# Layer 2 of an attention + two-layer MLP kernel: plain block products against one-level Strassen on 768-token groups

## The chip, the cores and the metric

The kernel runs on one core of a Trainium2 chip. The metric is the device time of one execution in microseconds (us).

## What is computed

Attention with a causal mask and a cumulative bias over 4 batches, 8 heads, 576 positions and head size 64, then two MLP layers on the 2304 tokens (d_model 512, d_ff 2048):

```python
x = attn_out.transpose(0, 2, 1, 3).reshape(2304, 512)
h = x @ w_in;    x = (h * clip(h + 3, 0, 6) / 6) @ w_out      # layer 1
h = x @ w2_in;   y = (h * tanh(log1p(exp(h)))) @ w2_out       # layer 2
```

All inputs are float32. The kernel keeps the precision with pairs of float32r tiles: each operand is split into a high part (a rounding cast) and a low part (the difference), and a product is three matmuls, high x high, high x low and low x high (`TERMS`). The weights arrive as 64-bit words and are rebuilt to float32 on the chip.

## The kernel before, in words

Tokens are processed in five blocks, `BLOCKS` (line 24), of 512 or 384 columns. A step is one block with one of the 16 slices `f` of d_ff. In `moe_step` (line 726) a step of layer 2 does G1, line 735: 4 chunks of d_model x 3 terms = 12 matmuls of N columns into one PSUM bank; then Mish on ScalarE (line 753), the high cast (line 755, made by `copy`, line 303 or 307) and the low difference on VectorE (line 756); then G2, line 773: N/128 x 3 matmuls of 512 columns that accumulate over the 16 slices in PSUM. Layer 1 has the same form with lines 735 and 768; its G2 has 4 x 3 matmuls of N columns. G1 of a later step stands between the groups of G2 of an earlier one, three matmuls by three.

`load_split` (line 341) brings a slice of weights (512 KB of words, `wraw`), rebuilds it in four VectorE or ScalarE operations (`wtmp`, lines 352 to 368) and splits it (lines 377 and 378). Layer 1's `w_out` slices are written to DRAM (`wos`, line 403) and read again per step into three `wo` buffers (line 406). Layer 2's slices all stay on the chip.

The order of each engine's work is made ahead of time by a planner (`Plan`, line 67) from costs, priorities and due times (table `T`, line 34). Attention (`unit` and `small`) runs beside layer 1: its operations on VectorE, ScalarE and GpSimd stand between the MLP's. During the first part of the program the planner fills idle time of TensorE with dummy matmuls (`warm`, line 293).

## Time and profile before

| what | us |
|---|---|
| median of 3 runs | 1002.57 (1002.32 to 1002.92) |
| profiled execution, first to last instruction (span) | 999.2 |
| TensorE busy in it | 987.7 |
| VectorE busy | 462.9 |
| ScalarE busy | 475.6 |
| GpSimd busy | 44.4 |

For the profiled execution the profile gives the span and no other time; the 3.4 us between it and the median of the runs is what lies around the span. A busy time counts an engine while any of its instructions is open. A matmul's own duration is longer than the distance from its start to the next one's start, because matmuls overlap in the engine; the pace is read from starts. VectorE operations overlap by their ends in the same way.

### The profile page before, as it was taken

The page shows a single profiled execution, that of the slowest core. Times are in us where ns is not written, and L with a number is a line of the kernel's source. Part 1 is how long each engine was busy: PE and PEld are TensorE (multiplying, and loading weights), DVE is VectorE, ACT ScalarE, POOL GpSimd, SP SyncE. Part 2 cuts the span into 40 slices and gives each one's busy share as a digit, 9 for nine tenths or more (in the row PEclk, how much of TensorE's full clock was granted, in tenths as well). Part 3 has the DMA queues.
Part 4 walks back from the last instruction along what each step waited for, and adds up shares of the span by engine and source line. Part 5 has one row for each costly group of instructions (what it writes and reads, how often), then busy time and mean ns, then how long its engine had stood idle before and what let it go on. Part 6 is the DMA issues. An engine that isn't in the chain of part 4 may idle for free.

```text
span 999.2 us, 14034 instructions
## 1 busy us (share of the span) xinstructions
PE 987.7 (99%) x5142; PEld 810.7 (81%) x5142; DVE 462.9 (46%) x1067; ACT 475.6 (48%) x1008; POOL 44.4 (4%) x102
## 2 busy tenths in 40 slices
PE   8899999999999999999999999999999999999998
PEld 6567777777777898888889998888888888888996
DVE  7898888754544455435228789612112112111111
ACT  5887777766655565544226556313223223222222
POOL 2111110101011001000000000000000000000000
PEclk9999999999999999999999999999999999999999
DMA  8786876887566766466237775202001102000101
GB/s 276 221 251 223 277 242 229 262 262 223 170 202 201 236 211 207 146 230 221 90 121 258 258 269 177 81 1 74 1 1 43 43 1 63 1 1 1 43 1 32
DMA packets 60356, 146.06 MB, mean 146 GB/s; under 512 B 8352, under 2 KB 22720, under 8 KB 60288
## 3 DMA queue, kind: packets, MB, share of 16 engines
q1 hardware_dynamic: 60288, 145.17, 44.8%
q8 instruction: 41, 0.67, 0.3%
q14 instruction: 27, 0.22, 0.1%
HBM read 121.84 MB, written 23.31 MB: 145 GB/s over the span
## 4 chain that ended last, share of the span: by engine, by line
PE 97%; DVE 2%; ACT 1%; issue 0%; POOL 0%; POOLq 0%; DVEq 0%; ACTq 0%
PE b L735 40%; PE b L768 21%; PE b L773 20%; PE b L499 4%; PE b L568 4%; PE b L545 3%; PE b L623 2%; PE b L293 1%; PE b L677 1%; PE b L668 1%; DVE g L635 0%; ACT cb L642 0%; DVE wtmp L362 0%; DVE cb L635 0%; DVE win L378 0%
## 5 line engine op out<-in xcount | busy, mean ns | idle before, releaser
L735 PE MATMUL b<-blk,win 128*128 128x512 f32 (+1 forms) x1920 | 505.3, 373 | 0.0
L735 PEld LDWEIGHTS b<-blk,win 128*128 128x128 f32 x1920 | 347.1, 188 | 58.0 <-issue 6.9
L768 PE MATMUL b<-g,wo 128*128 128x512 f32 (+1 forms) x960 | 258.6, 377 | 0.0
L768 PEld LDWEIGHTS b<-g,wo 128*128 128x128 f32 x960 | 170.3, 188 | 28.4 <-issue 8.2
L756 DVE TENSOR_TENSOR g<-e,g 128x512 fp32r<-128x512 f32 (+1 forms) x120 | 77.0, 642 | 215.4 <-ACT g L303 214.4
L753 ACT ACTIVATE e<-b 128x512 f32<-128x512 f32 (+1 forms) x80 | 44.4, 555 | 249.2 <-PE b L735 249.0
L773 PE MATMUL b<-wo,wo 128*128 128x512 f32 x432 | 122.0, 391 | 0.0
L773 PE MATMUL b<-wo,g 128*128 128x512 f32 x432 | 122.0, 391 | 0.0
L303 ACT ACTIVATE g<-e 128x512 fp32r<-128x512 f32 (+1 forms) x105 | 62.2, 593 | 78.4 <-PE b L768 76.8
L773 PEld LDWEIGHTS b<-wo,g 128*128 128x128 f32 x432 | 80.5, 188 | 13.3 <-DVE g L756 0.3
L773 PEld LDWEIGHTS b<-wo,wo 128*128 128x128 f32 x432 | 80.6, 188 | 12.9
L756 DVE TENSOR_TENSOR wo<-e,wo 128x512 fp32r<-128x512 f32 (+1 forms) x40 | 25.5, 638 | 131.6 <-ACT wo L303 131.4
L748 DVE SCALAR_TENSOR_TENSOR e<-e,b 128x512 f32<-128x512 f32 (+1 forms) x80 | 50.4, 629 | 59.4 <-ACT e L746 58.5
L514 ACT ACTIVATE cb<-cb,nm 128x384 f32<-128x384 f32 (+2 forms) x80 | 54.4, 682 | 29.7 <-DVE nm L506 29.0
L746 ACT ACTIVATE e<-b,three 128x512 f32<-128x512 f32 (+1 forms) x80 | 51.4, 642 | 32.3 <-DVE g L756 16.2
L506 DVE CUSTOM_DVE_ANT_0 cb<-b,cb 128x384 f32<-128x384 f32 (+2 forms) x80 | 44.7, 588 | 29.6 <-PE b L499 25.6
L303 ACT ACTIVATE pt<-b 128x384 f32<-128x384 f32 (+2 forms) x95 | 47.8, 504 | 19.5 <-PE b L545 18.5
L545 PE MATMUL b<-ident,cb 128*128 128x128 f32 x304 | 48.8, 272 | 0.0
L545 PEld LDWEIGHTS b<-ident,cb 128*128 128x128 f32 x304 | 39.0, 140 | 9.2
L499 PE MATMUL b<-qk 64*128 64x384 f32 (+2 forms) x288 | 46.2, 364 | 0.0
L362 DVE SCALAR_TENSOR_TENSOR wtmp<-wraw,wtmp 128x512 uint32<-128x512 uint32 x64 | 44.2, 691 | 1.2
L368 DVE SCALAR_TENSOR_TENSOR wtmp<-wraw,wtmp 128x512 uint32<-128x512 uint32 x64 | 44.0, 687 | 1.0
(79 smaller groups left out, 744.0 us busy)
## 6 DMA issues: line engine op xcount, KB each, us to landing
wo<-wos SPq DMA_DIRECT2D x64, 512.0 KB, 3.7
wraw<-in_w_in_dram SPq DMA_DIRECT2D x32, 512.0 KB, 4.9
wraw<-in_w_out_dram SPq DMA_DIRECT2D x32, 512.0 KB, 4.4
cb<-cuml SPq DMA_DIRECT2D x16, 896.0 KB, 7.6
wos<-wo SPq DMA_DIRECT2D x16, 512.0 KB, 4.9
qkr<-in_qk_dram SPq DMA_DIRECT2D x16, 480.0 KB, 3.6
v<-in_v_dram SPq DMA_DIRECT2D x16, 320.0 KB, 6.4
cb<-cums SPq DMA_DIRECT2D x12, 384.0 KB, 4.5
```

The costliest lines, as they stand in the source:

```text
L303: nc.scalar.activation(out=out_, in_=in_, func=AF.Copy)
L499: nc.tensor.matmul(out=ps[g].t[:, 0:w], lhsT=t.t[s_, ka, qo:qo + P], rhs=t.t[s_, kb, nk0 + a:nk0 + e], start=k == 0, stop=k == 2)
L506: nc.vector.tensor_tensor_reduce(out=p.t[:, o:o + w], in0=pb.t[:, 0:w], in1=cb.t[:, o:o + w], scale=-0.125, scalar=(3.0e38 if a == 0 else ...
L514: nc.scalar.activation(out=p.t[:, o:o + w], in_=p.t[:, o:o + w], func=AF.Exp, scale=-1.0, bias=nm.t[:, k:k + 1], accum_out=l.t[:, k:k + 1],)
L545: nc.tensor.transpose(out=ps.t[:, P * z:P * (z + 1)], in_=p.t[:, o:o + P], identity=ident)
L735: nc.tensor.matmul(out=hps.t[:, 0:N], lhsT=w.t[:, a, P * c:P * (c + 1)], rhs=x.t[:, c, b, :], start=(c == 0 and k == 0), stop=(c == NCC - ...
L746: a = add("ACT", actp(N, 1), lambda: nc.scalar.activation(out=e0.t[:, 0:N], in_=hps.t[:, 0:N], func=AF.Relu, bias=three, scale=1.0), [prev ...
L748: a = add("DVE", v1x(N), lambda: nc.vector.scalar_tensor_tensor(out=e0.t[:, 0:N], in0=e0.t[:, 0:N], scalar=6.0, in1=hps.t[:, 0:N], op0=ALU ...
L753: a = add("ACT", actp(N) + 0.15, lambda: nc.scalar.activation(out=e0.t[:, 0:N], in_=hps.t[:, 0:N], func=AF.Mish), [prev], t, [e0], [hps])
L756: gl = add("DVE", v1x(N), lambda: nc.vector.tensor_tensor(out=g.t[:, 1, 0:N], in0=src.t[:, 0:N], in1=r(g.t[:, 0, 0:N]), op=ALU.subtract), ...
L768: nc.tensor.matmul(out=y[j].t[:, 0:N], lhsT=wt.t[:, a, P * j:P * (j + 1)], rhs=g.t[:, b, 0:N], start=(f == 0 and k == 0), stop=(f == NF - ...
L773: nc.tensor.matmul(out=y[j].t, lhsT=g.t[:, a, P * j:P * (j + 1)], rhs=wt.t[:, b, :], start=(f == 0 and k == 0), stop=(f == NF - 1 and k == 2),
```

## The change

Layer 2 is computed on three groups of 768 tokens (`SUPER`), each group in a G1 part and then a G2 part. In both parts the matrices are cut into 2 x 2 blocks: d_model into halves, d_ff into halves (slice `f` with slice `f + 8`), tokens into halves of 384 (`NS`). Seven block products with sums of blocks take the place of eight (the Winograd form). In G1 a product is 6 matmuls of 384 columns for one of 8 slice pairs; in G2 it is 8 x 6 matmuls over the slice pairs, into two banks. One chain (`last_pe`) sets the order of the products on TensorE.

- **Weights.** `combine_in` (for `w2_in`) and `combine` (for `w2_out`) rebuild two slices, form the block sums with four VectorE operations of 256 columns, and write seven blocks to DRAM (`wss`): `w2_in` as float32 (three writes, 896 KB for a slice pair), `w2_out` split already (one write of 1792 KB). The first runs beside attention, the second late in layer 1. `granule` reads one block per product: 128 KB in G1, split on the chip, 256 KB in G2.
- **Tokens.** `operands` reads layer 1's output of the group, forms four sums and splits seven operands of 768 columns. In G2 `op` forms sums of the Mish outputs for four of the seven products and splits each operand of 384 columns.
- **Partial results.** A bank is read (`snap`, a copy, or `psum_add`) in the middle of its accumulation, and later products go on accumulating in it.
- **Layer 1 and attention** keep their work. The planner's table `T` has other numbers, transfers are reckoned at 330 instead of 270 KB per us, `qkr` has one buffer instead of two, and `small` keeps its input in `v`. The output is written as 512 x 2304, and its axes are put in order on the host.

```diff
 LA = 2
+NS = 384
+SUPER = [0, 768, 1536]
+KP = NF // 2
...
-    sm=3.895, sm2=5.532, w0=5.919, w1=9.308, cum=14.045, wo=0.564, blk0=27.645, blk1=12.97, wo2=44.236,
...
+    sm=1.176, sm2=5.532, w0=5.919, w1=9.308, cum=14.045, wo=0.564, blk0=27.645, blk1=12.97, wo2=44.236, wo2r=11.75,
...
-    return nbytes / 270e3
+    return nbytes / 330e3
...
+    def combine_in(f, prio, deps):
+        G = Buf("G1", [P, 3, 2 * P], F32)
+        X, x = rebuild(w2_in[f], prio, deps, (), (), lambda: None)
+        Y, y = rebuild(w2_in[f + KP], prio, deps, (), (), lambda: None)
...
+            n.append(add("DVE", v1x(2 * P), lambda o=o, a=a, b=b, op=op: nc.vector.tensor_tensor(
+                out=o(), in0=a(), in1=b(), op=op), [n[-1], x], prio, new, uses))
...
+    def combine(k, f, prio, deps):
+        G = Buf("G", [P, 7, 2, 2 * P], F32R)
...
+        for a, e in ((0, 4), (4, 7)):
...
+        e = add("SP", 0.5, lambda: nc.sync.dma_start(out=wss[k][f][:], in_=r(G.t)), ends, prio, (), [G], lat=dma(P * 14336))
...
+    def granule(k, p, f, prio, deps):
+        b = Buf("ws", [P, 2, 2 * P], F32R)
+        if k:
+            return b, [add("SP", 0.5, lambda: nc.sync.dma_start(out=r(b.t), in_=wss[k][f][:, SLOT[p]]), [*wss_n[k, f], *deps], prio, [b],
+                           lat=dma(P * 2048))]
...
+        def g1(p, f, bank, start, stop):
+            w, nw = granule(0, p, f, at[0] - T["lead"] * d, [n2])
...
+                for j in range(2):
+                    for k, (a, b) in enumerate(TERMS3):
+                        nc.tensor.matmul(out=bank.t[:, 0:NS], lhsT=w.t[:, a, P * j:P * (j + 1)], rhs=xo[p].t[:, j, b, :],
...
+            n1 = g1(1, f, X, True, True)
+            if pend:
+                pend()
...
+            c1 = snap(X, s1, n1, t)
+            n = g1(2, f, Y, True, True)
+            c = psum_add(lambda s1=s1: s1.t, Y, lambda s1=s1: s1.t, [n, c1], t + d, (), [s1])
+            mish(s1, f, 0, c, t + 2 * d)
+            n = g1(6, f, X, False, True)
+            c2 = snap(X, s2, n, t + 2 * d)
+            n5 = g1(5, f, Z, True, True)
+            n = g1(7, f, X, False, True)
+            c3 = snap(X, s3, n, t + 4 * d)
...
+                    for m in range(2):
+                        for k, (a, c) in enumerate(TERMS3):
+                            nc.tensor.matmul(out=banks[m].t[:, 0:NS], lhsT=w.t[:, a, P * m:P * (m + 1)], rhs=b.t[:, c, :],
...
+        n = g2(1, bx, True)
+        c1 = [snap(bx[m], s1[m], n, at[0]) for m in range(2)]
+        n5 = g2(5, bz, True)
+        n = g2(6, bx, False)
```

**The order on TensorE in layer 2** (`win` weights and `blk` tokens of G1, `g` or `wo` operands of G2). Before:

```order
L735 MATMUL b_7186<-blk,win 128x512 x3
L773 MATMUL b_6889<-wo_6402,wo 128x512 x3
L735 MATMUL b_7186<-blk,win 128x512 x3
L773 MATMUL b_6897<-wo_6402,wo 128x512 x3
L735 MATMUL b_7186<-blk,win 128x512 x3
```

Of the change, with what each waits for, in G1 of the first group (the bank is ahead of the arrow; `xob` and `blk` hold token operands, the second name the weight block):

```order
L922 MATMUL b_6521<-xob,wsb 128x384 [waits Activation_49]
L922 MATMUL b_6521<-xob,wsb 128x384 x5
...
L922 MATMUL b_6545<-xob,blk 128x384 [waits DVE_49]
L922 MATMUL b_6545<-xob,blk 128x384 x5
L922 MATMUL b_6521<-xob,st 128x384 [waits Activation_49]
L922 MATMUL b_6521<-xob,st 128x384 x5
L922 MATMUL b_6567<-xob,st 128x384 [waits DVE_49]
L922 MATMUL b_6567<-xob,st 128x384 x5
L922 MATMUL b_6521<-blk 128x384 [waits Activation_49]
L922 MATMUL b_6521<-blk 128x384 x5
```

Groups of three that alternated between G1 and G2 are now groups of six of one product. Bank `b_6521` holds product 1, then 1 + 6, then 1 + 6 + 7; between 6 and 7 stands one other product, and 7 waits for ScalarE, which reads the bank in between.

**The order on VectorE at the start of G2 of the first group** (`L868` and `L882` make the next group's token operands, `L983`, `L986` and `L970` the sums of Mish outputs, `L992` the low part of an operand of G2). Before, a step of layer 2 had one such operation, line 756. Now:

```order
L882 TENSOR_TENSOR xob<-wraw,xob 128x2x384
L882 TENSOR_TENSOR xob<-xob 128x2x384
L882 TENSOR_TENSOR blk<-xrb,blk 128x2x384 x2
L882 TENSOR_TENSOR xob<-wraw,xob 128x2x384
L882 TENSOR_TENSOR xob<-xob 128x2x384
L992 TENSOR_TENSOR blk<-win,blk 128x384
L983 TENSOR_TENSOR win<-win 128x384
L986 TENSOR_TENSOR win<-win 128x384 x2
L992 TENSOR_TENSOR blk<-win,blk 128x384 x3
```

Six splits of 768 columns for the next group stand in one piece ahead of operands that this G2 takes.

**The order of transfers on SyncE early in layer 1's second block** (`wo<-wos` are the weights that each step takes). Before:

```order
L406 DMA wo<-wos_114 128x1024
L403 DMA wos_129<-wo 128x1024
L476 DMA v<-in_v_dram 128x2x320
L581 DMA xs_3_85<-st 128x320 x2
L406 DMA wo<-wos_115 128x1024
L795 DMA ys_0_94<-st 128x512
```

Now:

```order
L434 DMA wo<-wos_108 128x1024
L397 DMA wraw<-in_w_in_dram 128x512
L542 DMA v<-in_v_dram 128x2x320
L647 DMA xs_3_79<-st 128x320
L431 DMA wos_123<-wo 128x1024
L647 DMA xs_3_79<-st 128x320
L454 DMA ws_1_93<-wtmp 128x512
L397 DMA wraw<-in_w_in_dram 128x512
L838 DMA ys_88<-st 128x512
L434 DMA wo<-wos_109 128x1024
```

Between two reads of `wos` there are now reads of layer 2's words (`wraw`) and writes of its blocks (`ws`), and a write waits on the same queue until its sums are made.

## Rows read from the trace of the kernel before

**Rows 1.** The page: engines busy, the chain that ended last, by engine and line.
```profile
PE 987.7 (99%) x5142; PEld 810.7 (81%) x5142; DVE 462.9 (46%) x1067; ACT 475.6 (48%) x1008; POOL 44.4 (4%) x102
...
PE 97%; DVE 2%; ACT 1%; issue 0%; POOL 0%; POOLq 0%; DVEq 0%; ACTq 0%
```

**Rows 2.** Groups by shape on TensorE: line, operands, count, busy us, mean ns.
```profile
L735 PE MATMUL b<-blk,win 128*128 128x512 f32 x1152 | 330.6, 396 | 0.0
L735 PE MATMUL b<-blk,win 128*128 128x384 f32 x768 | 174.7, 339 | 0.0
...
L773 PE MATMUL b<-wo,wo 128*128 128x512 f32 x432 | 122.0, 391 | 0.0
L773 PE MATMUL b<-wo,g 128*128 128x512 f32 x432 | 122.0, 391 | 0.0
```

**Rows 3.** TensorE in order of time, layer 2, 512-column block: start, us, what.
```profile
700.57 0.84 PE L773 MATMUL b<-wo,wo 128*128 128x512 f32 x3
701.25 0.84 PE L735 MATMUL b<-blk,win 128*128 128x512 f32 x3
```

**Rows 4.** The same view, layer 2, 384-column block; 16 pairs between the first and last.
```profile
769.80 0.69 PE L735 MATMUL b<-blk,win 128*128 128x384 f32 x3
770.33 0.86 PE L773 MATMUL b<-wo,g 128*128 128x512 f32 x3
...
789.38 0.69 PE L735 MATMUL b<-blk,win 128*128 128x384 f32 x3
```

**Rows 5.** The same view, end of layer 1, all matmuls of 384 columns.
```profile
559.69 0.68 PE L768 MATMUL b<-g,wo 128*128 128x384 f32 x3
560.21 0.68 PE L735 MATMUL b<-blk,win 128*128 128x384 f32 x3
...
567.49 0.68 PE L735 MATMUL b<-blk,win 128*128 128x384 f32 x3
```

**Rows 6.** Groups by shape on VectorE and ScalarE: count, busy us, mean ns.
```profile
L756 DVE TENSOR_TENSOR g<-e,g 128x384 fp32r<-128x384 f32 x48 | 26.7, 557 | 72.8 <-ACT g L303 72.4
...
L460 DVE TENSOR_TENSOR qk<-qkr,qk 128x960 fp32r<-128x960 f32 x16 | 18.5, 1157 | 3.3 <-ACT qk L303 2.9
...
L753 ACT ACTIVATE e<-b 128x384 f32<-128x384 f32 x32 | 15.7, 491 | 96.1 <-PE b L735 96.1
```

**Rows 7.** VectorE in order of time, end of layer 1: start, us, what.
```profile
573.45 0.56 DVE L756 TENSOR_TENSOR g<-e,g 128x384 fp32r<-128x384 f32 x1
573.93 0.68 DVE L368 SCALAR_TENSOR_TENSOR wtmp<-wraw,wtmp 128x512 uint32<-128x512 uint32 x1
```

**Rows 8.** The end of the program in order of time: start, us, what.
```profile
990.20 0.69 PE L735 MATMUL b<-blk,win 128*128 128x384 f32 x3
...
990.93 0.49 ACT L753 ACTIVATE e<-b 128x384 f32<-128x384 f32 x1 [2.44 <-PE b L735]
...
992.01 0.56 DVE L756 TENSOR_TENSOR g<-e,g 128x384 fp32r<-128x384 f32 x1 [2.93 <-ACT g L303]
...
992.62 1.45 PEld L773 LDWEIGHTS b<-wo,g 128*128 128x128 f32 x7 [0.30 <-DVE g L756]
```

**Rows 9.** Stretches: length, busy PE, PEld, DVE, ACT, POOL, clock, DMA share, GB/s.
```profile
70.00:80.00 10.00, 10.00 (x50) 7.24 (x51) 8.91 (x23) 7.89 (x21) 2.94 (x4) 1.00 0.95 264
110.00:120.00 10.00, 10.00 (x51) 7.50 (x51) 7.14 (x19) 6.59 (x19) 1.48 (x4) 1.00 1.01 345
150.00:200.00 50.00, 50.00 (x269) 38.04 (x268) 39.16 (x90) 38.07 (x82) 5.15 (x10) 1.00 0.75 246
200.00:300.00 100.00, 100.00 (x558) 75.24 (x557) 50.19 (x125) 64.09 (x136) 7.80 (x20) 1.00 0.69 214
...
540.00:580.00 40.00, 40.00 (x233) 40.00 (x232) 32.63 (x58) 21.95 (x39) 0.00 (x0) 1.00 0.80 271
```

**Rows 10.** Transfers: what, count, KB each, median us from issue to landing.
```profile
wo<-wos SPq DMA_DIRECT2D x64, 512.0 KB, 3.7
...
blk<-ys SPq DMA_DIRECT2D x12, 256.0 KB, 3.9
```

More of the change, by code (lines that the diff above doesn't have):

```diff
@@ L99, in can @@
                 need[b.tag] = need.get(b.tag, 0) + 1
-        if not all(self.slots.get(k, 1) >= v for k, v in need.items()):
+        if not all(len(self.slots.get(k, ())) >= v for k, v in need.items()):
             return False
@@ L339, in setup_cum, with rebuild @@
             )
-    def load_split(buf, layer, src, prio, deps=(), gate=()):
-        raw = Buf(main_p, "wraw", [P, DM], I64)
-        tmp = Buf(main_p, "wtmp", [P, DM], F32)
+    def rebuild(src, prio, deps, new, uses, dst, after=()):
+        raw = Buf("wraw", [P, DM], I64)
+        tmp = Buf("wtmp", [P, DM], F32)
         def words():
@@ new lines, in combine @@
+    def combine(k, f, prio, deps):
+        G = Buf("G", [P, 7, 2, 2 * P], F32R)
+        lo = lambda a: r(G.t)[:, a, 1, :]
+        src = (w2_in, w2_out)[k]
+        rows = ((slice(0, 2), slice(2, 4)), (slice(0, 3, 2), slice(1, 4, 2)))[k]
+        n = [None, None]
+        for h in range(2):
+            _, n[h] = rebuild(src[f + KP * h], prio, deps, [] if h else [G], [G],
+                              lambda h=h: lo(rows[h]), n[:h])
+        for o, a, b, op in ((5, 0, 2, ALU.subtract), (2, 2, 3, ALU.add), (4, 2, 0, ALU.subtract), (6, 1, 4, ALU.subtract)):
+            n.append(add("DVE", v1x(2 * P), lambda o=o, a=a, b=b, op=op: nc.vector.tensor_tensor(
+                out=lo(o), in0=lo(a), in1=lo(b), op=op), [n[-1], n[0]], prio, (), [G]))
+        ends = []
+        for a, e in ((0, 4), (4, 7)):
+            w = 2 * P * (e - a)
+            h = add(("ACT", "DVE"), (act(w), v2x(w)), lambda q, a=a, e=e: copy(q, G.t[:, a:e, 0, :], r(G.t)[:, a:e, 1, :]), [n[-1]], prio, (), [G])
+            ends.append(add("DVE", v1x(w), lambda a=a, e=e: nc.vector.tensor_tensor(
+                out=G.t[:, a:e, 1, :], in0=r(G.t)[:, a:e, 1, :], in1=r(G.t)[:, a:e, 0, :], op=ALU.subtract), [h], prio, (), [G]))
+        e = add("SP", 0.5, lambda: nc.sync.dma_start(out=wss[k][f][:], in_=r(G.t)), ends, prio, (), [G], lat=dma(P * 14336))
+        wss_n[k, f] = [e]
+        return e
@@ L755, in moe_step @@
[L755 removed]
+        e0 = Buf("e0", [P, 512], F32)
+        a = add("ACT", actp(N, 1), lambda: nc.scalar.activation(
+            out=e0.t[:, 0:N], in_=hps.t[:, 0:N], func=AF.Relu, bias=three, scale=1.0), [prev], t, [e0], [hps])
+        a = add("DVE", v1x(N), lambda: nc.vector.scalar_tensor_tensor(
+            out=e0.t[:, 0:N], in0=e0.t[:, 0:N], scalar=6.0, in1=hps.t[:, 0:N], op0=ALU.min, op1=ALU.mult), [a], t, (), [e0, hps])
@@ L756, in moe_step @@
+        gh = add(("ACT", "DVE"), (act(N), v2x(N)), lambda e: copy(e, g.t[:, 0, 0:N], e0.t[:, 0:N]), [a], t, [g], [e0])
         gl = add("DVE", v1x(N), lambda: nc.vector.tensor_tensor(
-            out=g.t[:, 1, 0:N], in0=src.t[:, 0:N], in1=r(g.t[:, 0, 0:N]), op=ALU.subtract), [gh], t, (), [g, src])
-        nj = NCC if layer == 0 else N // P
+            out=g.t[:, 1, 0:N], in0=e0.t[:, 0:N], in1=r(g.t[:, 0, 0:N]), op=ALU.subtract), [gh], t, (), [g, e0])
         if f == 0:
-            ypst[layer, i] = [Bank([j]) for j in range(nj)]
@@ new lines, in phase, with grant, turn @@
+        def phase(tag, prio, deps, *sizes):
+            b = Buf(tag, [P, MAP[tag][2] // 4], F32)
+            n = add("X", 0.0, lambda: None, deps, prio, [b])
+            b.users.add(None)
+            def grant():
+                got, off = {}, 0
+                for k, m, size in sizes:
+                    got.setdefault(k, []).extend((b, off + size * i) for i in range(m))
+                    off += m * size
+                return got
+            n.grant = grant
+        def turn():
+            stack.close()
+            pools["late"] = stack.enter_context(tc.tile_pool(name="late", bufs=1))
@@ new lines, in tile_attention_moe_moe @@
+        n2 = add("X", 0.0, turn, all_att, pos[NF * 3])
+        end = LB + T["g"] + 4
+        phase("xob", LB, [n2], ("xo", 5, 16 * NS))
+        phase("xrb", LB, [n2], ("xr", 3, 8 * NS))
+        phase("ub", LB, [n2], ("u", 3, 4 * NS))
+        phase("wsb", LB, [n2], ("ws", 2, 2048))
+        phase("blk", pos[NF * 4] - T["blk0"] + 0.1, [n2], ("xo", 2, 16 * NS), ("ws", 2, 2048))
+        phase("blk", LB, [n2], ("ao", 5, 8 * NS))
+        for tag, sizes in (("g", [("ao", 1, 8 * NS)]), ("wo", [("yu", 2, 4 * NS)]), ("e0", [("yu", 1, 4 * NS)]), ("st", [("ws", 1, 2048)])):
+            for _ in range(MAP[tag][1]):
+                phase(tag, end, [n2], *sizes)
@@ new lines, in tile_attention_moe_moe @@
+        for k in range(2):
+            for f in range(KP):
+                e = (combine if k else lambda _, *x: combine_in(*x))(k, f, LB - T[f"c{k}"] + T[f"cs{k}"] * f, [n2 if k else n0])
+            phase("G" if k else "G1", LB - T[f"c{k}"] + T[f"cs{k}"] * KP, [e], ("ws", 7, 2048) if k else ("u", 2, 4 * NS))
+        for _ in range(2):
+            phase("wraw", end, [e], ("xr", 1, 8 * NS))
+            phase("wtmp", end, [e], ("ws", 1, 2048))
+        d = 6 * mm_cost(NS) / 1.36
+        at = LB + T["gap"]
```

493 lines of the change are left out of this document (316 added, 177 removed).

## The prediction

> **What bounds the kernel now.** First the page's chain of waits and its busy times: TensorE is open 987.7 us of 999.2, and 97% of the chain runs through it [rows 1]. So a saved microsecond of TensorE is a saved microsecond of the kernel, as long as nothing else comes late. Next the groups by shape [rows 2]: line 735 serves both layers, 1152 matmuls of 512 columns and 768 of 384, half of each in layer 2; line 773 is layer 2's G2, 864 matmuls of 512. Their mean durations (391 and 396 ns) are not their price, since matmuls overlap; that is the distance between starts, in the timeline. Three matmuls of 512 columns follow each other every 0.68 us [rows 3]; a pair of three at 384 and three at 512 takes 1.224 us (769.80 to 789.38 is 16 pairs) [rows 4]; where all have 384 columns, three take 0.52 us [rows 5]. Last the table by stretches, for the room on VectorE and the DMA queues: at the end of layer 1 TensorE keeps exactly this pace while VectorE is busy 32.63 of 40 us and DMA 0.80 [rows 5, 9]. Layer 2 comes after that and leaves both nearly idle, which is the room that the change uses.
>
> **What the change removes: TensorE time in layer 2.** Before: 3 blocks x 16 steps x 8 groups of three at 0.68 = 261.1 us [rows 3]. A step of a 384-column block has four groups of 384 and three of 512, so 3 pairs of 1.224 and one group of 0.52 = 4.19 us [rows 4, 5]; 32 of them are 134.1. Together 395.2 us. After: the built order has 1008 matmuls at G1's line and 1008 at G2's, all of 384 columns, so 672 groups of three at 0.52 = 349.4 us. The matmuls become more (2016 for 1824), the columns 7/8. **Gain 45.8 us.** That the program does not do what it says is excluded by these counts.
>
> **What it adds inside layer 2.** *VectorE in G2.* With the first three of the seven products of G2 in groups 0 and 1 stand, by the order, 34 operations of 384 columns and 10 of 768 (sums, low parts, and the next group's token operands). TensorE needs 24 x 1.04 = 25.0 us for those products. A 384-column operation lasts 557 ns [rows 6], but the next one starts 0.48 us after it [rows 7]; for 768 columns I read between 384 (557) and 960 (1157) 0.96 us, and 0.87 from start to start with the same overlap. That makes 34 x 0.48 + 10 x 0.87 = 25.0 us at the pace of rows 7, and 34 x 0.557 + 10 x 0.96 = 28.5 at full durations. So VectorE is as long as TensorE there, and every late operand holds the chain of products; between 0 and 3.5 us a group, I take 2, nearer to the overlapped pace but not at it, since many operations wait for a ScalarE cast in between: **+4 us** for two groups (the third has no next group's operands). Weighed against it, the Trainium skill (VectorE: DVE Perf Modes, "The TRN2 errata") says that an operation that reads SBUF pays a fixed latency each time, so that many small tiles pay it often, and gives a lone fp32 tensor_tensor as (N+151)/0.96 ns, an estimate of 557 for 384. The duration agrees with rows 6; rows 7 show that a queued neighbour does not pay all of it. By the rule alone the term would be 7 instead of 4.
>
> *Banks read in the middle, in G1.* Product 7 goes on in the bank that ScalarE copies after product 6, with one product (1.04 us) between. A group of three ends 0.16 us after the next begins (0.68 against 0.52) [rows 5]; ScalarE starts 0.04 after the end of the matmul (990.20 + 0.69 against 990.93), a read of 384 columns lasts 0.49, and TensorE starts 0.05 after the engine it waits for (992.57, 992.62) [rows 6, 8]. The sum, 0.74, fits in 1.04. If another ScalarE operation of 0.49 stands wholly ahead, 0.19 us is missing. There are 48 such places (products 6 and 7, 24 slice pairs), so 0 to 9 us; ScalarE has some 14 operations in the 7.3 us of a slice pair, so I take a third: **+3 us**. The waits on transfers cost nothing while blocks are read ahead: the order has up to 16 blocks in hand or on their way.
>
> *Turns between the parts.* Six times the next part needs banks that VectorE has just read: +0.2 us each, **+1 us** (0 to 3). The end is as before: copy or sum, then a store.
>
> **What it moves into layer 1.** Rebuilding `w2_in` (16 slices, four operations each), its sums and its writes now run beside attention, `w2_out` in the stage after it. Per slice pair SyncE gets two reads of 512 KB and three writes; behind a write that waits for its sum stand reads of `wos`. Those have three buffers, so about two steps (2 x 5.44 us) of room, less 3.7 us to land [rows 10]: 7 us late is hidden, more is not. The load on DMA: over some 150 us (about 150 to 300) 246 x 50 + 214 x 100 = 33.7 MB flow now [rows 9]; the change adds 16 x 0.52 + 8 x 0.92 = 15.7 MB. At the best rate that rows 9 show (345 at share 1.01, so 342 GB/s; 271 at 0.80 gives 339) 49.4 MB takes 144 us, at the worst (264 at 0.95, so 278) 178. So the queue is nearly full, and the price is 0 to 28 us. The load on VectorE rises there from 89 of 150 us by at most 51 (three operations of rebuilding for each of 16 slices at 0.68 [rows 7], and 32 sums, each shorter than the 0.56 of 384 columns) to 94%; but stretches with 39.16 of 50 and with 50.19 of 100 let through nearly the same stream of matmuls (269 in 50, 558 in 100) [rows 9], so I price that at nothing by itself and leave it to the end of the range. I take **+5 us**, near the best rate since what is added are plain rows of 1 KB and more; and as the attention's due times are new, a gain of 5 us is the other end.
>
> **Sum.** 999.2 - 45.8 + 4 + 3 + 1 + 5 = 966.4 us of span, plus the 3.4 us by which the median of the runs (1002.57) stands above the profiled span: **970 us**.
>
> **Rivals.**
> 1. *VectorE sets the pace of G2.* Its operations are short and most wait for ScalarE, so each costs its full duration or more. For: 28.5 against 25.0 us. Against: only three of seven products are so dense, and rows 5 and 9 show TensorE undisturbed at 82%. 3.5 a group, and 2 more for the products behind: 970 + 7 = 977 us.
> 2. *The DMA queue in layer 1 is over-full.* Writes wait on SyncE, `wos` reads come late, and TensorE stands between 150 and 300 us, and again while `w2_out` goes out. For: the 144 to 178 us above. Against: 7 us of room at each step. 970 + 23 = 993 us.
> 3. *The weight blocks come too slowly, and it is slower than before.* A G2 part reads 56 blocks of 256 KB (14.7 MB), tokens and stores add 3.1, and about 16 blocks (4.2 MB) are there at its start: 13.6 MB in 58.2 us, 234 GB/s. A 256 KB read takes 3.9 us to land [rows 10], 67 GB/s alone, so three must overlap all the time; at 180 GB/s each part takes 75.6 us, 17.4 more, and three make 970 + 52 = 1022 us. It decides at (58.2 + 11) us a part, 197 GB/s. Against it: rows 9 show 345 GB/s. The Trainium skill (DMA: Bandwidth & Descriptors, "Bandwidth") speaks for it: it asks for transfers of 1 MB or more for 75% of the peak, and has 138 GB/s at 64 KB and 341 at 1 MB (loads that GpSimd issued), with 256 KB in between. Rows 9 are of a mix of sizes up to 1 MB, so no row here shows a stream of 256 KB alone.
>
> **How the numbers follow.** Forecast 0.67; rival 1 0.12; rival 2 0.13; rival 3 0.08. The predicted time is the forecast's, 970. All added terms at nothing and the gain of 5 give 952, all bounds of layer 2 high and layer 1 as taken give 981; rival 2 reaches 993. For 8 in 10 I take 954 to 992. A difference of 0.2% (2 us) is what a measurement of this kernel can tell from none. Faster: forecast, rivals 1 and 2, less 0.02 for a mix of them, 0.90; same 0.02; slower 0.08.
>
> **What would show it.** Right: 2016 matmuls of 384 columns at 0.52 us a group of three; layer 2 some 357 us from its first product to the last; VectorE about full in the first half of G2 of groups 0 and 1, with small holes on TensorE there; DMA share above 0.85 between 150 and 300 us. Rival 1 shows as waits of line 1005 for line 992, rival 2 as gaps in lines 792 and 817 that end with `wo<-wos`, rival 3 as waits of line 1005 for `ws`. Wrong altogether: a group of three of 384 columns that takes more than 0.57 us without a wait, for at that pace the 672 groups cost 33 us more.

## The result and the profile after

The changed kernel takes **959.41 us** (median of 4 runs, 958.15 to 960.25) against 1002.45 us in the same comparison: ratio 0.958, 95% interval 0.9564 to 0.9596. The forecast was 970, faster.

The page of the changed kernel, the busy times and the chain of waits by engine:

```profile
span 958.4 us, 16307 instructions
...
PE 941.1 (98%) x5294; PEld 819.1 (85%) x5294; DVE 702.3 (73%) x1627; ACT 588.9 (61%) x1310; POOL 43.6 (5%) x102
...
PE 82%; DMA 5%; DVE 5%; ACT 2%; issue 1%; SPq 0%; ACTq 0%; DVEq 0%
```

Against [rows 1] TensorE is still busy for 98% of the span, VectorE has gone from 462.9 to 702.3 us and ScalarE from 475.6 to 588.9; the chain still runs mostly through TensorE. Layer 2 in the timeline of TensorE: its first product, one of its holes, and its last matmuls (start, us, engine, line, what, idle time before and what ended it).

```profile
595.86 1.20 PE L922 MATMUL b<-xob,wsb 128*128 128x384 f32 x6
...
670.72 1.20 PE L1005 MATMUL b<-g,st 128*128 128x384 f32 x6
671.76 1.20 PE L1005 MATMUL b<-g,blk 128*128 128x384 f32 x6
672.80 0.34 PE L1005 MATMUL b<-blk,st 128*128 128x384 f32 x1
673.49 1.56 PE L1005 MATMUL b<-blk,st 128*128 128x384 f32 x6 [0.36 <-DVE blk L992]
...
952.70 2.25 PE L1005 MATMUL b<-g,G 128*128 128x384 f32 x12
```

Six matmuls of 384 columns follow each other every 1.04 us (670.72, 671.76, 672.80), the 0.52 for three of [rows 5]. From 595.86 to the end of the last matmul (952.70 + 2.25) are 359.1 us, with 12 matmuls of layer 1 (2.1 us) among them; 357 was forecast. The holes in it, as the table of TensorE's waits lists them for layer 2 (the weight loads of PEld run ahead of the matmuls, so their waits show the whole delay; us in total, times, longest):

```profile
PEld b L1005 <- DVE blk L992: 2.9, 4, 1.1
PEld b L922 <- ACT G L321: 1.0, 2, 0.7
PEld b L922 <- DVE ub L898: 1.0, 2, 0.5
PEld b L922 <- ACT ub L321: 0.9, 2, 0.5
...
PEld b L1005 <- ACT blk L321: 0.6, 2, 0.3
PEld b L922 <- DVE G L898: 0.5, 1, 0.5
```

These are three kinds. G2 waits for operands that VectorE or ScalarE makes late: 2.9 + 0.6 = 3.5 us (forecast 4). G1 waits for ScalarE, which has not yet copied a bank: 1.0 + 0.9 = 1.9 (forecast 3). G1 waits for VectorE at three places, each the last product of a G1 part: 1.0 + 0.5 = 1.5 (forecast 1, at another place). No line waits for a transfer of `ws`.

The stretches that answer to [rows 9], with the first 25 us of G2 in the first two groups (columns as there):

```profile
200.00:300.00 100.00, 99.39 (x541) 75.65 (x541) 75.13 (x177) 67.64 (x139) 8.56 (x20) 1.00 0.97 331
658.20:683.20 25.00, 24.32 (x138) 23.45 (x137) 24.09 (x42) 16.58 (x33) 0.00 (x0) 1.00 0.88 286
777.50:802.50 25.00, 23.91 (x136) 23.04 (x135) 24.04 (x42) 16.05 (x32) 0.00 (x0) 1.00 0.83 272
```

VectorE's load between 200 and 300 us has risen from 50.19 to 75.13 us and DMA's share from 0.69 to 0.97, and yet layer 1 takes no longer. I measure it from the first to the 913th of the 960 matmuls of its G2 (line 768 before, 817 now; the last ones stand among layer 2): 68.4 to 589.9 us before, 71.1 to 589.1 now, so 521.5 and 518.0 us. (Ahead of the first one stand 12 more matmuls of line 792 now, 2.7 us at the pace of [rows 3]; with them it is 520.7, some 0.8 us less than before.) The forecast had charged 5 us here.

**Where the 43 us come from.** The span went from 999.2 to 958.4. The forecast's span was 966.4; of the 8.0 us between, layer 1 ends 0.75 us earlier instead of 5 later (5.75), the end of the program is 1.25 shorter, and the holes are 6.9 instead of 8 (1.1). The other 2.4 us of the 10.4 between 970 and 959.4 are in the 3.4 that the forecast put around the span.

### The profile page after: what moved, and what is told of

Read it like the earlier page. It is cut to its first block, busy times and chain, and to the rows that moved or that the text cites. A ratio compares the mean times of both kernels' runs of the same rounds, so it can differ in the third digit from the quotient of the medians.

```text
span 958.4 us, 16307 instructions
## 1 busy us (share of the span) xinstructions
PE 941.1 (98%) x5294; PEld 819.1 (85%) x5294; DVE 702.3 (73%) x1627; ACT 588.9 (61%) x1310; POOL 43.6 (5%) x102
## 4 chain that ended last, share of the span: by engine, by line
PE 82%; DMA 5%; DVE 5%; ACT 2%; issue 1%; SPq 0%; ACTq 0%; DVEq 0%
PE b L817 20%; PE b L792 19%; PE b L922 16%; PE b L1005 15%; PE b L565 4%; PE b L634 3%; PE b L611 3%; DMA wraw<-in_w_in_dram 3%; PE b L688 1%; DVE xob L882 1%; DMA G<-ws 1%; PE b L742 1%; DVE wtmp L393 1%; DMA wo<-wos 1%; DVE blk L992 1%
## 5 line engine op out<-in xcount | busy, mean ns | idle before, releaser
L792 PE MATMUL b<-blk,win 128*128 128x512 f32 (+1 forms) x960 | 235.0, 377 | 0.1
L792 PEld LDWEIGHTS b<-blk,win 128*128 128x128 f32 x960 | 170.0, 188 | 29.3 <-issue 8.3
L321 ACT ACTIVATE blk<-win 128x384 fp32r<-128x384 f32 x85 | 43.4, 522 | 26.6 <-PE b L1005 18.5
L1005 PE MATMUL b<-blk,G 128*128 128x384 f32 x312 | 57.1, 334 | 0.8 <-DVE blk L992 0.8
L992 DVE TENSOR_TENSOR blk<-win,blk 128x384 fp32r<-128x384 f32 x87 | 46.8, 552 | 11.6 <-ACT blk L321 11.3
L1005 PEld LDWEIGHTS b<-blk,G 128*128 128x128 f32 x312 | 54.3, 188 | 1.1 <-DVE blk L992 1.1
L922 PE MATMUL b<-xob,G 128*128 128x384 f32 x300 | 54.9, 335 | 0.2 <-DVE ub L898 0.2
L922 PEld LDWEIGHTS b<-xob,G 128*128 128x128 f32 x300 | 52.1, 188 | 0.7 <-DVE ub L898 0.5
L565 PE MATMUL b<-qk 64*128 64x384 f32 (+2 forms) x288 | 44.6, 364 | 0.6 <-DVE nm L572 0.6
L370 ACT ACTIVATE wtmp<-wraw 128x512 f32<-128x512 f32 x47 | 31.4, 668 | 22.0 <-DMA wraw<-in_w_in_dram 13.5
L380 DVE SCALAR_TENSOR_TENSOR wtmp<-wraw,wtmp 128x512 uint32<-128x512 uint32 x64 | 44.3, 693 | 0.8
```

Source lines behind the costliest of these rows:

```text
L321: nc.scalar.activation(out=out_, in_=in_, func=AF.Copy)
L565: nc.tensor.matmul(out=ps[g].t[:, 0:w], lhsT=t.t[s_, ka, qo:qo + P], rhs=t.t[s_, kb, nk0 + a:nk0 + e], start=k == 0, stop=k == 2)
L792: nc.tensor.matmul(out=hps.t[:, 0:N], lhsT=w.t[:, a, P * c:P * (c + 1)], rhs=x.t[:, c, b, 0:N], start=(c == 0 and k == 0), stop=(c == NCC ...
L922: nc.tensor.matmul(out=bank.t[:, 0:NS], lhsT=w.t[:, a, P * j:P * (j + 1)], rhs=xo[p].t[:, j, b, :], start=start and j == 0 and k == 0, sto ...
L992: l = add("DVE", v1x(NS), lambda: nc.vector.tensor_tensor(out=b.t[:, 1, :], in0=src(), in1=r(b.t)[:, 0, :], op=ALU.subtract), [h], prio, ( ...
L1005: nc.tensor.matmul(out=banks[m].t[:, 0:NS], lhsT=w.t[:, a, P * m:P * (m + 1)], rhs=b.t[:, c, :], start=start and f == 0 and k == 0, stop=f ...
```

## The experiments

Two lengths from the timeline of each kernel serve throughout: layer 1 as just defined, and layer 2 from the start of its first product to the end of the last matmul.

| kernel | median us | ratio to before, 95% | layer 1 | layer 2 |
|---|---|---|---|---|
| before | 1002.45 | 1 | 521.5 | |
| the change | 959.41 | 0.9564 to 0.9596 | 518.0 | 359.1 |
| new numbers alone, on before | 1000.52 | 0.9971 to 1.0011 | 516.4 | |
| change with all old numbers | 971.55 | 0.9667 to 0.9728 | 536.0 | |
| change with old pace and hop | 975.70 | 0.9729 to 0.9761 | 542.9 | |
| change with old pace alone | 970.94 | 0.9676 to 0.9710 | 535.3 | |
| extra traffic in layer 1 | 962.52 | 0.9569 to 0.9637 | 523.4 | 358.1 |
| no rebuilding of weights | 957.80 | 0.9531 to 0.9592 | 517.1 | 358.4 |
| less read-ahead | 958.42 | 0.9538 to 0.9595 | 517.4 | 355.8 |
| seven block buffers | 959.62 | 0.9564 to 0.9596 | 517.5 | 356.7 |
| product 4 twice | 1003.58 | 1.0010 to 1.0037 | 517.7 | 403.0 |
| operands due later | 957.03 | 0.9532 to 0.9585 | 517.9 | 356.3 |
| later, and no turn | 953.07 | 0.9501 to 0.9530 | 517.6 | 354.0 |
| later, no turn, weight splits later | 953.12 | 0.9510 to 0.9547 | 518.1 | 352.0 |

(With the old pace, in three kernels, layer 1 and layer 2 overlap by some 10 us more, so no length of layer 2 is given there. Their layer 1 holds 24, 24 and, with the pace alone, 18 matmuls of layer 2, 4.2 and 3.1 us, that the other kernels do not have in it.)

### Is layer 2 bound by TensorE alone?

```diff
+            times = 2 if p == 4 else 1
...
-                n = pe(fn, [*nw, *nb], banks if start and f == 0 else [], [*banks, w, b])
+                n = pe(fn, [*nw, *nb], banks if start and f == 0 else [], [*banks, w, b], times)
```

> The changed kernel with product 4 of G1 and of G2 run twice into its banks: eight products on TensorE where the change has seven, with VectorE's, ScalarE's and the transfers' work as it is (the output counts product 4 twice). Theory (TensorE is the bound in all of layer 2): 48 groups of six more in G1 and 48 in G2, 96 x 1.04 = 99.8 us in all, if a doubled product is one seventh of 349.4 us, 49.9 us in G1 and G2 together: 1007 to 1009 us, less at most 3 us of holes. Rival (the seven products are paced by something else, VectorE or the weight blocks): the added products fill holes, under 40 us more, below 1000 us.

(The first product in that text is a slip: product 4 has 24 groups of six in G1 and 24 in G2, 48 x 1.04 = 49.9, the number it goes on with.) Layer 2 grew by 44.0 us, the median by 44.2. The holes, taken as gaps between starts beyond the pace, shrank from 6.6 to 1.3 us, more than the 3 expected, since VectorE and ScalarE now have the time of eight products for the work of seven; 49.9 less 5.3 leaves 44.6. So an eighth product costs its full time on TensorE, and outside these holes nothing else paces layer 2.

### The holes in G2: VectorE's order or its capacity?

```diff
-        xo, xn = operands(si, pos - T["xo0"] if si == 0 else pos - KP * 7 * d + 4 * d)
+        xo, xn = operands(si, pos - T["xo0"] if si == 0 else pos - KP * 7 * d + 24 * d)
```

> The changed kernel with the token operands of the next group due 20 products later in G2 (24 in place of 4), so that by the order each sum of VectorE that G2's matmuls wait for stands at least 5 products ahead of them on its queue. Theory (the holes of the dense part come from VectorE's order alone, not from its capacity): the holes of G2 in groups 0 and 1, 3.4 us in the changed kernel, go, and the time is 2.5 to 3.5 us shorter, 956 us, with no wait of the line of G2's matmuls for VectorE over 0.3 us. Rival (VectorE has too little time there, 25.0 to 28.5 us of work in 25.0 of TensorE): the holes only move to the products behind, 2 to 4 us of them stay, the time is within 1 us of the changed kernel's.

TensorE's waits in layer 2 of this kernel, and the same first 25 us of G2:

```profile
PEld b L922 <- ACT ub L321: 1.7, 2, 1.5
PEld b L922 <- ACT G L321: 1.5, 3, 0.9
PEld b L922 <- DVE ub L898: 1.0, 2, 0.5
PEld b L922 <- DVE G L898: 0.5, 1, 0.5
```

```profile
659.10:684.10 25.00, 25.00 (x147) 25.00 (x146) 23.62 (x44) 17.34 (x34) 0.00 (x0) 1.00 0.92 302
777.40:802.40 25.00, 25.00 (x146) 25.00 (x145) 24.20 (x45) 17.59 (x34) 0.00 (x0) 1.00 0.88 287
```

Line 1005 waits for nothing any more. VectorE is nearly as full in these 25 us as before (23.62 and 24.20 us in 44 and 45 operations, for 24.09 and 24.04 in 42; in the first group 9 of them have 768 columns, for 11), and TensorE stands for none of it. The two G2 parts with holes take 58.24 us each instead of 59.71 and 60.15, 3.4 us less, all that was expected; layer 2 as a whole gained 2.8, since a hole in G1 grew by 0.9. The median is 2.4 us lower, but the intervals of the two kernels overlap; it is the trace that decides. VectorE's capacity was not the limit. In the change six splits of 768 columns (0.87 us from start to start, 5.2 us in all) stand in one piece ahead of an operand that G2 takes next; the first and the last of them:

```profile
667.68 0.95 DVE L882 TENSOR_TENSOR xob<-wraw,xob 128x768 fp32r<-128x768 f32 x1
...
672.02 0.95 DVE L882 TENSOR_TENSOR xob<-xob 128x768 fp32r<-128x768 f32 x1
672.89 0.55 DVE L992 TENSOR_TENSOR blk<-win,blk 128x384 fp32r<-128x384 f32 x1
```

The operand of 672.89 is ready at 673.44, and TensorE goes on at 673.49. The second hole of the group, at 675.37, is the next sum and operand behind the same piece.

### The hole at each end of G1

```diff
-        pend()
...
+                if p == 1 and f == 0:
+                    pend()
```

> As the kernel with the operands due later, and besides the last slice pair's product 3 of G1 is put behind the first six groups of three of G2's first product. Theory (the 0.47 us hole at each end of G1 is that product's wait for the bank that VectorE reads after product 7, since only one product stands between): three holes of 0.47, 1.4 us, go, and the time is 1.0 to 1.4 us below that of the kernel with the operands due later, 954 to 955 us. Rival (the hole is the turn to the next part's banks, as the prediction had it): the holes stay and move to G2's first matmuls, no difference over 0.5 us.

(The "six groups of three" in that text are six matmuls: in the trace product 3 stands one product, 1.04 us, further back.)

The waits for `DVE ub L898` and `DVE G L898` are gone; what is left in layer 2 is this:

```profile
PEld b L922 <- ACT G L321: 1.4, 3, 0.6
PEld b L922 <- ACT ub L321: 0.7, 1, 0.7
```

So the hole belonged to product 3 of the last slice pair, which goes on in a bank that VectorE reads after product 7, with one product between; it is not a turn to the next part's banks. The median fell by 4.0 us, more than the 1.0 to 1.4 expected. Layer 2 explains 2.3 of it (1.4 for the three holes, the rest smaller holes in G1). The rest fits the first 75 us of the program, which differ from run to run (layer 1 begins at 72.5 and 69.4 us in the two profiled ones; last section). This kernel beats the change: its interval lies wholly below.

### The holes in the middle of G1

ScalarE in the change, around one of them (TensorE goes on at 744.33, after the copy of 743.81):

```profile
742.00 0.42 ACT L321 ACTIVATE G<-G 128x256 fp32r<-128x256 f32 x1 [0.86 <-DMA G<-ws]
742.32 0.51 ACT L928 ACTIVATE win<-G 128x384 f32<-128x384 f32 x1
742.74 0.40 ACT L321 ACTIVATE wsb<-wsb 128x256 fp32r<-128x256 f32 x1
743.38 0.53 ACT L928 ACTIVATE win<-ub 128x384 f32<-128x384 f32 x1 [0.24 <-DVE ub L898]
743.81 0.47 ACT L321 ACTIVATE ub<-b 128x384 f32<-128x384 f32 x1
```

ScalarE stands at the split of a weight block that has not landed (742.00), and the bank copy stands behind it. (Between them the Mish of 743.38 waits 0.24 us for a sum of VectorE, which stood behind the low part of the same block.) Of the four places of this kind three look like this, with waits of 0.64 to 0.86 us for a block; the fourth, 0.3 us, has its cause in the last section. The experiment keeps the last kernel and lets the plan place such a split at least 2 us after it believes the block has landed:

```diff
-                    m.ready = max(m.ready, n.end + (0.0 if n.on == "SP" or n.on == m.eng[0] == "PE" else HOPS.get((n.on, m.eng[0]), 0.12) + HOP + m.slack))
+                    m.ready = max(m.ready, n.end + (m.slack if n.on == "SP" else 0.0 if n.on == m.eng[0] == "PE" else HOPS.get((n.on, m.eng[0]), 0.12) + HOP + m.slack))
...
-        return b, split(n, prio + T["slead"], b, (lambda: b.t[:, 0], lambda: b.t[:, 1]), 2 * P)
+        hl = split(n, prio + T["slead"], b, (lambda: b.t[:, 0], lambda: b.t[:, 1]), 2 * P)
+        hl[0].slack = 2.0
+        return b, hl
```

> As the kernel with later operands and no turn, and in the plan each of G1's weight blocks is split no sooner than 2 us after the plan believes it landed, so that on ScalarE fewer bank copies stand behind a split whose block is still on its way. Theory (the holes of 0.2 to 1.3 us that are left in the middle of G1 are bank copies that stand on ScalarE behind such a split): those holes, 1.6 us in all in the kernel with later operands and no turn, fall below 0.5 us, layer 2 takes 352.3 to 353.0 us in place of 353.97, and ScalarE's waits for weight blocks shrink. Rival (the bank copies come late by themselves, from the density of ScalarE's and VectorE's work at those places): the holes stay, 353.5 us or more.

The table lists one wait in the whole of layer 2, and ScalarE's waits for weight blocks fall from 22.8 us in the change to 4.3; the two largest lines:

```profile
PEld b L924 <- ACT G L321: 0.3, 1, 0.3
```

```profile
ACT st L321 <- DMA st<-ws: 1.8, 2, 1.1
ACT G L321 <- DMA G<-ws: 1.2, 1, 1.2
```

Layer 2 takes 352.0 us, below the 352.3 to 353.0 expected. Of these, 349.4 are the 672 groups of three, 2.1 are 12 matmuls of layer 1 that stand among them, 0.3 are holes, and 0.2 is the end of the last matmul beyond the pace. The median did not move (953.12 and 953.07), because this kernel's layer 1 began 1.6 us later in the profiled run (71.0 and 69.4 us), a scatter that other kernels show too.

### Do the weight blocks come fast enough?

```diff
-    pe=2.015, bias=2.4, la=3, la2=2, wp=11.079, p0=-8.796, p1=2.142, p2=3.12, p3=65.354, xo0=10.159, lead=10.412,
+    pe=2.015, bias=2.4, la=3, la2=2, wp=11.079, p0=-8.796, p1=2.142, p2=3.12, p3=65.354, xo0=10.159, lead=2.5,
```

> The changed kernel with the weight blocks of G2 due 2.5 us ahead of their product in place of 10.4. Theory (the stream of 256 KB blocks has room: a block lands in 3.2 us and several overlap): up to 2 us more than the changed kernel, 959 to 962. Rival (the stream needs all of its read-ahead, as the forecast's slower case assumed): waits of the line of G2's matmuls for the blocks, 10 us or more in all, 970 us and above.

The time fits the theory, but the experiment does not test it: SyncE issues the reads of line 889 as buffers come free, 16.4 to 16.9 us ahead of their use, whatever the due time. (The new due times changed VectorE's order as well, and 2.7 us of the holes in G2 went.) So the buffers were taken away instead:

```diff
-        for tag, sizes in (("g", [("ao", 1, 8 * NS)]), ("wo", [("yu", 2, 4 * NS)]), ("e0", [("yu", 1, 4 * NS)]), ("st", [("ws", 1, 2048)])):
+        for tag, sizes in (("g", [("ao", 1, 8 * NS)]), ("wo", [("yu", 2, 4 * NS)]), ("e0", [("yu", 1, 4 * NS)]), ("st", [("yu", 1, 4 * 384)])):
...
-            phase("G" if k else "G1", LB - T[f"c{k}"] + T[f"cs{k}"] * KP, [e], ("ws", 7, 2048) if k else ("u", 2, 4 * NS))
+            phase("G" if k else "G1", LB - T[f"c{k}"] + T[f"cs{k}"] * KP, [e], ("ws", 1, 2048) if k else ("u", 2, 4 * NS))
```

> The changed kernel with 7 in place of 17 buffers for layer 2's weight blocks, so that a read goes out about 7 products (7.3 us) ahead of its use in place of 16.4 to 16.9. (In the kernel with less read-ahead the buffers, not the due times, still set the distance: 16.4 us there too.) Theory (a block lands 3.2 to 3.6 us after its issue, and the queues hold the 252 GB/s of a G2 part): no wait of the line of G2's matmuls for a block, up to 3 us more in G1, where a block must be split after it landed; 959 to 963 us. Rival (the stream needs its depth, as the forecast's slower case assumed): waits of the line of G2's matmuls for blocks, 10 us or more in the three G2 parts, 970 us and above.

SyncE's queue and TensorE in the first G2: the block `G` whose read is issued at 688.72 is used at 694.77, 6.05 us later.

```profile
688.72 0.32 SPq L889 DMA_DIRECT2D G<-ws  x1
```

```profile
694.77 1.20 PE L1005 MATMUL b<-g,G 128*128 128x384 f32 x6
```

One line of the same part's transfers (KB each, median us from issue to landing), and its stretch:

```profile
wtmp<-ws SPq DMA_DIRECT2D x16, 256.0 KB, 4.0
```

```profile
659.00:717.50 58.50, 58.11 (x333) 57.25 (x332) 49.98 (x97) 33.51 (x68) 0.00 (x0) 1.00 0.88 280
```

The reads go out some 6 us ahead, a little less than the 7.3 expected. No matmul of G2 waits for a block in any of the three groups, and the time is that of the change. It is so by two effects that cancel. The holes of G2 fall from 3.5 to 1.3 us, as the plan orders VectorE differently here too, and those of G1 that wait for a bank copy rise from 1.9 to 4.7, as the theory had it for blocks that must be split after they landed:

```profile
PEld b L922 <- ACT ub L321: 3.5, 5, 1.4
```

Blocks of 256 KB come at 280 GB/s with 6 us of read-ahead; the slower case, which needs under 197 GB/s, is excluded by a wide margin.

### What the load moved into layer 1 costs

First the new planner numbers without the load, and the load without the numbers:

```diff
...
-    wo2r=11.978, win2=5.088, g=30.578, upre=6.511, uhalf=1.145, upost=3.306, uv=0.304, spre=6.035, shalf=0.728,
-    spost=1.158, pe=5.322, bias=2.302, la=3, la2=2, wp=11.079, p0=-8.796, p1=2.0, p2=2.856,
+    wo2r=11.75, win2=5.088, g=30.578, upre=6.511, uhalf=1.737, upost=3.306, uv=0.304, spre=6.035, shalf=-0.675,
+    spost=1.158, pe=2.015, bias=2.4, la=3, la2=2, wp=11.079, p0=-8.796, p1=2.142, p2=3.12,
...
-    return nbytes / 270e3
+    return nbytes / 330e3
```

> The kernel before, with nothing of the change but its new planner numbers (due times, the pace assumed for transfers, no allowance between two steps of TensorE); both layers' matmuls as before. Theory (the load that the change moves into layer 1 is hidden, and the new numbers are worth little there): 1002 us, within 2 of the kernel before, and the last step of layer 1 within 1 us of where it was. Rival (the added load costs some 5 us, and the new numbers win them back, so that the sum came out near nothing): 996 to 998 us, with the end of layer 1 about 5 us earlier.

> The changed kernel with the planner numbers of the kernel before. Theory (the added load is hidden whatever the numbers): 959 to 963 us, end of layer 1 within 2 us of the changed kernel's. Rival (the load costs and the new numbers pay for it): layer 1 ends 5 us or more later, 965 to 970 us, with gaps before the matmuls of attention's lines that end with transfers of wos.

Neither theory holds as it was put. On the kernel before, the numbers change nothing that can be measured (1000.52 against 1002.14 us in the same comparison, interval from 0.9971 to 1.0011). With the load they are worth 12.1 us (971.55 against 959.41). With the old numbers the load lengthens layer 1 from 521.5 to 536.0 us, of which 4.2 are the 24 matmuls of layer 2, so by some 10; with the new ones from 516.4 to 518.0. The rival's mechanism is there, a load that the numbers pay for, but with other sizes than it gave, and without its sign: in the kernel with the old numbers no gap of TensorE ends with a transfer of `wos`. The largest group ends with nothing that the profile shows ("issue"), the rest with ScalarE and, 0.9 us, with VectorE:

```profile
PE b L611 <- issue: 3.7, 5, 1.9
PE b L634 <- ACT pt L321: 1.7, 2, 1.2
```

Which number it is, in two steps; first the pace of transfers and the allowance between TensorE's steps (`hop`) together, then the pace alone (the edit without its first two lines):

```diff
-                    m.ready = max(m.ready, n.end + (0.0 if n.on == "SP" or n.on == m.eng[0] == "PE" else HOPS.get((n.on, m.eng[0]), 0.12) + HOP + m.slack))
+                    m.ready = max(m.ready, n.end + (0.0 if n.on == "SP" else HOPS.get((n.on, m.eng[0]), 0.12) + HOP + m.slack))
...
-    return nbytes / 330e3
+    return nbytes / 270e3
```

> The changed kernel with two of the new planner numbers undone: the pace assumed for transfers (270 in place of 330 GB/s) and the allowance between two steps of TensorE. The due times stay the new ones. The change with all old numbers took 971.6 us, 14.5 us of it lost in layer 1 against the kernel before. Theory (the due times and lead factors of attention's stages pay for the load): under 3 us more than the changed kernel, up to 962. Rival (the plan's pace of transfers makes the difference, since it decides how early a read is believed to land): 968 to 972 us.

> The changed kernel with one planner number undone: the pace that the plan assumes for transfers, 270 in place of 330 GB/s. With pace and TensorE's allowance both undone it took 975.7 us, 21.4 us of it lost in layer 1 against the kernel before. Theory (the pace does it: 49.4 MB in the 150 us that the forecast spoke of are 183 us at 270 GB/s, so the plan itself believes the queue over-full and puts the work in another order, while the chip's queue is not full): 968 to 977 us, layer 1 10 to 21 us longer, and its gaps end with ScalarE or VectorE, none with transfers of wos. Rival (the allowance between two steps of TensorE does it): 959 to 963 us.

One number, the pace that the plan assumes, costs 11.5 us (970.94 against 959.41). With `hop` undone as well it is 975.70, above the rival's 968 to 972 and above the kernel with all old numbers (971.55), so the numbers act on each other and their costs do not add up. In the kernel with the old pace alone two gaps of TensorE, 5.0 us, end with a read of layer 1's tokens (`blk<-xs`), none with `wos`; the rest ends with ScalarE and VectorE or is spread over the stages. The longest, 3.06 us, ends at 340.74. From 340.1 the granted clock was at the lower level (1.2 GHz), after TensorE had been busy for 2.68 of the 5.1 us before:

```profile
340.10:346.90 6.80, 6.16 (x19) 6.16 (x20) 2.78 (x5) 1.69 (x3) 0.00 (x0) 0.50 1.02 403
```

The 36 matmuls of 384 columns from 340.74 take 9.17 us in place of 6.24 at the pace of [rows 5], so some 3 us of this profiled execution are the clock. The stretch of the forecast, in the change and in the kernel with the old pace:

```profile
150.00:300.00 150.00, 149.39 (x809) 112.57 (x808) 117.67 (x284) 106.42 (x228) 14.83 (x32) 1.00 0.91 312
```

```profile
150.00:300.00 150.00, 146.45 (x794) 110.12 (x793) 107.94 (x265) 98.48 (x214) 13.97 (x32) 1.00 0.84 280
```

With the old pace TensorE, VectorE and ScalarE do less in the same time while the DMA queues have more room (0.84 for 0.91). So over this stretch it is not the chip's queue that is over-full. A reason that fits, and that was only argued: the plan adds up bytes over pace on one queue; 49.4 MB are 183 us at 270 GB/s in these 150 us, so in the plan reads land late and everything behind them is placed late, while on the chip 46.8 MB (312 GB/s x 150 us) went through at a share of 0.91. Before the change 33.7 MB were 125 us, so the same pace did no harm. That any other disturbance of this plan might also cost some us is not excluded; the numbers alone on the kernel before cost nothing.

Then the queue itself, and the rebuilding:

```diff
+            nc.sync.dma_start(out=raw.t, in_=src)
+            if also is not None:
+                nc.sync.dma_start(out=also[:], in_=src)
...
+        X, x = rebuild(w2_in[f], prio, deps, (), (), lambda: None, (), idle[f])
```

> The changed kernel; each of the 16 raw slices of layer 2's w2_in is, right behind its read, copied once more within DRAM by the same queue (8.4 MB read and 8.4 MB written that nothing uses, between about 100 and 300 us). Nothing of the computation is changed. Theory (the queues are nearly full there but have room at each step): under 3 us more than the changed kernel, the DMA share of that stretch at or above 1. Rival (the queue stands at its edge, so what is added is paid): 16.8 MB at 330 to 342 GB/s is some 50 us of queue, of which 100 to 300 us holds at most 10 us idle, so 20 to 45 us more, with gaps before the matmuls of attention's lines that end with transfers of wos.

The median rose by 3.1 us, at the edge of the theory's 3; layer 1 of the profiled execution, the slowest of the four (965.95 us), by 5.4. So 8.4 MB more read and as much written are nearly hidden. The rate rose with them:

```profile
200.00:250.00 50.00, 48.05 (x257) 36.28 (x256) 36.50 (x82) 33.36 (x68) 3.49 (x8) 1.00 1.01 376
```

376 GB/s, where the best row before had 345 at the same share [rows 9]; but here the queue does bite: TensorE stands for 1.95 of 50 us. Of TensorE's waits in layer 1 only 0.5 us end with a transfer of `wos`, though; a late transfer comes by way of ScalarE and VectorE. The longest gap of layer 1, at 299.02:

```profile
296.50 0.67 ACT L371 ACTIVATE wtmp<-wraw 128x512 f32<-128x512 f32 x1 [4.13 <-DMA ws<-wtmp]
297.21 0.43 DVE L377 TENSOR_SCALAR wtmp<-wtmp 128x512 uint32<-128x512 uint32 x1 [3.06 <-ACT wtmp L371]
299.02 1.06 PE L570 MATMUL b<-qk 128*128 128x288 f32 x3 [1.89 <-DVE nm L577]
```

ScalarE stands 4.13 us for a write of a weight block that still holds its buffer, VectorE behind ScalarE (297.21), and the operation that TensorE waits for (line 577) behind that on VectorE.

```diff
+            if skip:
+                nc.gpsimd.memset(tmp.t if out_ is None else out_, 1.0)
+                return
...
-        X, x = rebuild(w2_in[f], prio, deps, (), (), lambda: None)
+        X, x = rebuild(w2_in[f], prio, deps, (), (), lambda: None, skip=True)
```

> The changed kernel without the rebuilding of layer 2's weights: the 32 raw slices of w2_in and w2_out are neither read nor converted on ScalarE and VectorE, GpSimd fills the tiles with a constant instead (left out: layer 2's real weights; the sums and the writes of the weight blocks stay). Theory (that work is hidden in layer 1): within 2 us of the changed kernel, 957 to 961, end of layer 1 within 1 us. Rival (it costs some of the 5 us that were forecast): 5 us or more faster, 952 to 955, all of it before the end of layer 1.

957.80 us, 1.6 below the change, with intervals that overlap; layer 1 0.9 us shorter. VectorE's load between 150 and 300 us falls from 117.67 to 94.11 us, and that buys next to nothing: the rebuilding is hidden.

## Why the prediction was right, and where its terms were off

**The gain of 45.8 us** is right. The groups of three take 0.52 us, and the kernel with one hole left shows the whole: 352.0 us, less 2.1 of layer 1, 0.3 of holes and 0.2 at the end, is the forecast's 349.4. Before the change, from the 913th matmul of layer 1's G2 (589.85) to the end of the last one (994.51) are 404.7 us; 48 matmuls of layer 1 take 8.3 of them, which leaves 396.3 for the forecast's 395.2.

**VectorE in G2, +4 us.** Measured 3.5. The place is right (the first half of G2, groups 0 and 1), the reason half right. I had it as capacity, 25.0 us of work in 25.0, with late operands as its effect. VectorE is indeed full (24.09 of 25 us), but with the operands due later the same work leaves TensorE without a hole. It is the order: operands stood behind 5.2 us of splits that nobody needed yet. That the size came out so near is in part luck. The rule that I weighed against it, that each short operation pays its fixed latency (the Trainium skill, VectorE: DVE Perf Modes, "The TRN2 errata"), would have made the term 7; the trace does not agree, as 44 operations go by in 25 us with TensorE never waiting in the kernel with the operands due later, and splits of 768 columns that last 0.95 us start every 0.87.

**Banks read in the middle of G1, +3 us.** Measured 1.9, by another mechanism. I expected one long ScalarE operation ahead of the copy at a third of 48 places. At 44 of the 48 the copy is in time, as the prediction's 0.74 against 1.04 us said. The holes are at four places, and at three of them ScalarE stands before a weight block that has not landed. The step that failed is the sentence "The waits on transfers cost nothing while blocks are read ahead": TensorE never waits for a block itself, but ScalarE's queue hands the wait on.

**Turns between the parts, +1 us.** Measured 1.5, but at three places, not six, and not where I put it: it is product 3 of the last slice pair of G1.

**Layer 1, +5 us.** Measured -0.75 by its end and some -0.8 by its length, so nothing. The size of the load was right (46.8 MB at a share of 0.91, 343 GB/s at a full share, the best rate that I took), and VectorE's load there, up by 28 us (89.35 to 117.67) for at most 51, costs nothing, as I priced it. What I missed is that the load and the plan's numbers act together: some 10 us with the old ones, 1.6 with the new.

**The end, 0.** I wrote "The end is as before"; it is 1.25 us shorter. From the end of the last matmul to the end of the program were 4.7 us and are 3.5. SyncE's last stores, four before and two now:

```profile
993.78 2.23 SPq L805 DMA_DIRECT2D out_dram<-st  x4
...
955.04 0.86 SPq L1013 DMA_DIRECT2D out_dram<-wo  x2
```

The last is issued 1.5 us after the last matmul's end (994.51) before and 0.95 (954.95) now; the other 0.7 us is what comes after, 3.2 and 2.5 us.

**Around the span, +3.4.** This was the distance of one profiled execution to a median of others, and part of it was chance: where the record has both for one execution, the time stands 1.7 to 2.6 us, mostly 1.8, above its span (960.25 and 958.4 for the change), and the change's median stands 1.0 above the profiled span.

**The rivals.** Rival 1 named the right sign, waits of line 1005 for line 992, but they are the forecast's own small term; VectorE sets no pace. Rival 2 did not come: one gap ends with `wo<-wos`, 0.3 us at 597.37, and even 8.4 MB more read and written cost 3 us. Yet the plan with 270 KB per us loses 11.5 us, for a reason that was only argued. Rival 3 did not come; the rule behind it (the Trainium skill, DMA: Bandwidth & Descriptors, "Bandwidth": 1 MB or more for three quarters of the peak) did not decide here: with several blocks on their way the part got the 280 GB/s that it asked for, most of it in reads of 256 KB. How much more such a stream could carry no run shows.

## What to carry to other kernels

Where one engine is the bound, fewer columns on it are worth their full time, provided that the engines that feed it have the right thing at the head of their queues: a busy share of 97% (24.20 of 25 us) harmed nothing, operands behind 5.2 us of early work did. A late transfer can reach the bound engine through a third engine's in-order queue, so a wait that no table shows against a DMA may still come from one; place an operation on transferred data some time after the expected landing. When traffic is added to a planned kernel, bring the plan's transfer rate up to what the trace shows before judging the change; here the old rate hid 11.5 of 43 us.
